# Moved and split steps at the start, in the scan and at the end of a Mamba-2 plus mixture-of-experts kernel

## The chip, the core and the metric

The kernel runs on one core of one Trainium2 chip. The metric is the device time of one execution in microseconds. Engines are called TensorE (PE; PEld is its weight loads), VectorE (DVE), ScalarE (ACT), GpSimd (POOL) and SyncE (SP); each works through its own queue in the order in which the program lists its instructions.

## The reference

Two stages follow each other. The first is a chunked state-space scan over 4 batches, 8 heads, 768 tokens, head size 32, state size 16:

```python
cum = np.cumsum(la, axis=-1)
L = np.exp(cum[:, :, :, None] - cum[:, :, None, :]) * causal
y_intra = einsum('bhij,bhjd->bhid', (C @ B.T) * L, x)
y_inter = einsum('bhin,bhnd->bhid', C, state) * np.exp(cum)[..., None]
state = decay_full * state + sum_j(B_j x_j * decay_from_j)
```

The second stage routes the 3072 resulting rows of 256 numbers to 8 experts by the largest cosine logit, and computes

```python
h = np.maximum(x[mask] @ w1[e], 0.0)
out[mask] = gate_w[mask, None] * (h @ w2[e])
```

with hidden size 1024; gate_w is the softmax value of the chosen expert. All is float32.

## The kernel before

The order of all work around the change is written out by hand: the program is recorded under a manual schedule, so the order of the calls is the order on each engine's queue.

**The scan.** It goes over NC = 6 chunks of Q = 128 tokens, all batches and heads together. For each chunk c, `spread_decays` (line 208) spreads the decays over the partitions by TensorE, into columns 384 to 512 of the PSUM tile `pg`; `scale_c` (268) multiplies them into C and gives `cp`; `mask_c` makes two masked copies on ScalarE. `inner(c, j)` (371) computes the scores of two batches (j = 0 for batches 0 and 1, j = 1 for 2 and 3) into columns 0 to 384 of `pg`, and `mask_inner(c, j)` (387, instruction line 391) multiplies the causal mask in on VectorE and gives `g`. As there is one `pg`, `inner(c, 1)` waits for the mask of (c, 0). `from_states` (397), `outputs` (408, line 419) and `first_outputs` (426, line 432) add up the outputs in the PSUM banks `py`: from the carried state, from the second 64 tokens with the scaled inputs `xs`, and from the first 64 tokens with `xb`. `xs` and `xb` are made on GpSimd (`scale_x` 290, `scale_first_half` 302) from `rT`, the turned inverse decays (`turn_inverses` 247). `sums`, `add_sums` and `decay_states` keep the state: products into the banks `pz`, `V` and the decayed `T` on VectorE. `between` (316) makes the factors between chunks, `wb` and `wm`. `keep_outputs` copies `py` to SBUF on ScalarE, and `finish` (452) turns the rows through `pz` and `py`, computes the logits with the turned expert embedding (`turn_emb`, `scale_emb`), and the rows go to DRAM.

In a chunk, `first_outputs` of all four batches stands behind `outputs(c, 1)`, which needs the mask of (c, 1). In the head of `mamba` (824), chunk 1's decays go to `pg` after chunk 0's have been read, then comes one warm-up matmul; on VectorE `scale_emb` stands ahead of the first mask, and `scale_c(1)` and `between` behind it, ahead of the second mask.

**The end of the scan.** `scan_end` (971) begins the first expert's first rows (`first.up`, `first.down`; each `f` is a 128 block of the hidden size) while the last chunk's rows are ranked within their experts. `rank_rows` is a small product, `keep_ranks` a copy, `places` a row of small VectorE operations, `locate` products that gather row indices in `pz`. `end_places` finishes the table, from which GpSimd gathers the rows of the job `late`.

**The experts.** The eight experts, the last six of them sorted by their number of rows, run as jobs, most of them with first-layer and second-layer products built from sums of blocks (lines 1244 and 1316). The last job has 364 rows in four tiles of `tr` = 104 (the last has 52). Its second layer is in `moe_end` (1505): `down(j, half)` computes 128 of the 256 output columns for rows 0 to 208 (half 0) or 208 to 364 (half 1), with one matmul pair for each of 8 values of f. Each `out(i)` turns a tile of rows back on TensorE (line 1361), scales it with the gate (1364 on ScalarE, 1366 on VectorE), and scatters it with an indirect DMA of GpSimd (1367).

Loads come by SyncE's queue in the order of the calls: a, then ct, bi, x, xa, b of chunk 0, then the same of chunk 1; later ones wait until their buffer is free (two buffers each).

Of the kernel before, what the change touches and what calls it, by code (L numbers as in the profile page):

```python
# [12 lines left out]
ALU = mybir.AluOpType  # L13
# [165 lines left out]
def warm_up(k, n):  # L179
    for _ in range(n):  # L180
        k.nc.tensor.matmul(k.pz[1][:], lhsT=k.warm[:, 0:Q], rhs=k.warm[:], start=True, stop=True)
# [23 lines left out]
    tt(out=v, in0=v, in1=w[:, 1].unsqueeze(3).to_broadcast([128, 2, 2, SQ]), op=ALU.mult)  # L205


def spread_decays(k, c):

    for b in range(NB):  # L210
        r = slice(32 * b, 32 * b + 32)
        k.nc.tensor.matmul(
            k.pg[:, b, 384:512], lhsT=k.spread[r, c % 4, :], rhs=k.f[r, c // 4, 0:Q], start=True, stop=True,
            tile_position=(32 * b, 0),
        )


# [50 lines left out]
def scale_c(k, c):  # L268


    t = k.ld[c]
    t.cp = k.work.tile([128, NB, 5, HQ], F32, name="cp", tag="cp")
    k.nc.vector.tensor_tensor(
        out=t.cp[:, :, 0:2, :].rearrange("p b j s -> p b (j s)"), in0=t.ct[:], in1=k.pg[:, :, 384:512], op=ALU.mult
    )
# [147 lines left out]
                    )  # L423


def first_outputs(k, c, zs=range(KD)):
    t = k.ld[c]
    for b in range(NB):
        for z in zs:
            for r in range(2):  # L430
                q, o = 2 * z + r, 64 * r
                k.nc.tensor.matmul(  # L432
                    k.py[z][o : o + 64, Q * b : Q * b + HQ],
                    lhsT=k.xb[c % 2][:, b, q].rearrange("p v d -> p (v d)"), rhs=t.g[b // 2][:, q, b % 2, 0:HQ],
                    start=False, stop=True, tile_position=(0, o), skip_group_check=True,
                )
# [127 lines left out]
def turn_emb(k, ps):  # L564


    nc = k.nc
    for z in range(KD):
        nc.tensor.transpose(ps[:, E * z : E * z + E], k.en2[:, z, :], k.ident[:E, :E])
    nc.scalar.copy(out=k.emb_t[:, :, 0:E], in_=ps[:, 0 : KD * E].rearrange("p (z e) -> p z e", z=KD))  # L570
# [253 lines left out]
def mamba(k):  # L824
    nc = k.nc
    k.f = k.mc.tile([128, 2, Q], F32, name="f")
    k.fe = k.mc.tile([128, 2, 3], F32, name="fe")
    k.rT = k.mc.tile([128, 2, 2, 128], F32, name="rT")
    k.V = k.mc.tile([128, NB, 2 * D], F32, name="V")
    k.ends = k.mc.tile([128, 8, NB, 3], F32, name="ends")  # L830
    k.rr, k.wm = {}, {}
    for c in range(NC):
        k.ld[c] = Net()
        k.ld[c].g = []
    load_decays(k)
    expert_emb(k)
    load(k, 0)
    build_consts(k)
    warm_up(k, 12)
    decays(k)  # L840
    load(k, 1)
    square_emb(k)
    clear_first_half(k, 0)
    clear_first_half(k, 1)
    route_consts(k)
    spread_decays(k, 0)
    warm_up(k, 3)
    split_b(k, 0)
    scale_c(k, 0)
    mask_c(k, 0)  # L850
    inverses(k, 0)
    block_ends(k)
    scale_emb(k)
    spread_decays(k, 1)
    warm_up(k, 1)
    inner(k, 0, 0)
    mask_inner(k, 0, 0)
    turn_inverses(k, 0, k.py[0][:, 0:256])
    scale_x(k, 0, nc.gpsimd)
    scale_first_half(k, 0, nc.gpsimd)  # L860
    scale_c(k, 1)
    spread_ends(k, k.pz[0][:, 0:96])
    between(k, 1, NC)
    turn_emb(k, k.pz[1][:, 400:416])

    for c in range(NC):
        t = k.ld[c]
        n = c + 1
        if c == 0:
            load(k, 2, ("ct", "x", "xa", "b", "bi"))  # L870
        elif c + 2 < NC:
            load(k, c + 2, ("x",))
        if 2 <= c < NC - 1:
            spread_decays(k, n)
        if 2 <= c < NC - 1:
            add_sums(k, c)
        if c >= 2:
            inner(k, c, 0)
        if c == NC - 1:
            finish(k, c - 1, (0,))  # L880
            early_places(k, c - 3)
        if c >= 2:
            mask_inner(k, c, 0)
# [12 lines left out]
        if 1 <= c < NC - 1:  # L896
            scale_c(k, n)
        if c >= 2:
            pick(k, c - 2)
        if c > 0:  # L900
            finish(k, c - 1, (2,) if c == NC - 1 else (1, 2) if 3 <= c else (0, 1, 2))
            keep_rows(k, c - 1)
            if c < NC - 1:
                send_rows(k, c - 1)
        inner(k, c, 1)
        mask_inner(k, c, 1)
        if c > 0 and n < NC:
            decay_states(k, n)
        if c > 0 and c + 2 < NC:
            load(k, c + 2, ("bi", "xa"), t.masked)  # L910
        if c == 0:
            sums(k, 0)
        if n < NC:
            split_b(k, n)
            mask_c(k, n)
            pass_c(k, n)
        if c == NC - 1:
            k.early_x = half_rows(k)
            gather_tiles(k, k.early_x, k.gi0, 0, 3 * NB * Q)
        if c >= 2:  # L920
            count_picks(k, c - 2)
        if c == NC - 1:
            add_located(k, c - 3)
        if c == 0:
            scale_first_half(k, n, nc.gpsimd, (0,))
        elif n < NC:
            scale_first_half(k, n, nc.gpsimd, after=t.paired)
        if 3 <= c < NC - 1:
            add_located(k, c - 3)
        if c > 0:  # L930
            from_states(k, c)
        if c >= 2:
            rank_rows(k, c - 2)
            keep_ranks(k, c - 2)
        outputs(k, c, 0)
        if c == 0:
            spread_decays(k, 2)
            inner(k, 1, 0)
            add_sums(k, 0)
            decay_states(k, 1)  # L940
            mask_inner(k, 1, 0)
        for zs in ((0,), (1,)) if c == NC - 1 else (range(KD),):
            outputs(k, c, 1, zs)
            first_outputs(k, c, zs)
            keep_outputs(k, c, zs)
        if c > 0 and c + 2 < NC:
            load(k, c + 2, ("b",), t.kept)
        if c == NC - 2:
            load_first_w1(k, 1, t.kept)
        if c == NC - 1:  # L950
            hold(k, send_rows(k, c - 1), t.kept)
            load_weights(k, 0, (1,), t.kept)
        if c + 2 < NC:
            sums(k, n)
        if c == 2:
            turn_inverses(k, 1, k.pz[0][:, 0:256])
        if c == NC - 1:
            pick(k, c - 1)
            count_picks(k, c - 1)
        if c >= 2:  # L960
            places(k, c - 2)
        if c == 4:
            shift_places(k)
        if c == 1:
            inverses(k, 1)
        if c == 0:
            scale_first_half(k, n, nc.gpsimd, (1,))
            place_consts(k)


def scan_end(k):
# [12 lines left out]
    gather_tiles(k, whole.x[:, 0:HT], k.gi0, NT, 3 * NB * Q)  # L984
    for f in range(3):
        first.up(f)
    locate(k, c - 2, True, False)
    first.up(3)
    rank_rows(k, c)
    keep_ranks(k, c)  # L990
    places(k, c)
    locate(k, c - 1, False, False)
    gates.square(0)
    first.up(4)
# [2 lines left out]
    for f in (5, 6, 7):  # L997
        first.up(f)
    locate(k, c, False, True)
    first.down(0, fs=range(2))  # L1000
    late = end_places(k, whole)
    first.down(0, fs=range(2, KF))
    gates.largest()
    gates.scale()
    gates.exp()
# [103 lines left out]
class Job:  # L1109
# [52 lines left out]
        else:  # L1162
            nc.vector.tensor_scalar_max(s.hT[:, f, 0:m], t, 0.0)

    def down(s, j, half=None, fs=range(KF)):
        k, nc, m = s.k, s.k.nc, s.cols
        if j == 0 and not half:
            s.yT = s.tile([128, KD, s.nt * s.tr], "yoT", 2 if s.p is None else 1)
        h = s.nt // 2 * s.tr
        r = slice(0, m) if half is None else slice(h * half, h + (m - h) * half)  # L1170
        if fs[0] == 0:
            s.yp = s.bank("yp", 4)
        t = s.yp[:, r]
        for f in fs:
            nc.tensor.matmul(  # L1175
                t, lhsT=s.w2[:, f, 128 * j : 128 * j + 128], rhs=s.hT[:, f, r], start=(f == 0), stop=(f == KF - 1)
            )
        if fs[-1] < KF - 1:
            return
        if j % 2 == 0 or s.bank_ is not None:  # L1180
            nc.scalar.copy(out=s.yT[:, j, r], in_=t)
        else:
            nc.vector.tensor_copy(out=s.yT[:, j, r], in_=t)
# [320 lines left out]

def moe_end(k, j):

    j.down(0, 0)
    j.down(1, 0)
    for i in range(2):
        j.down(0, 1, range(4 * i, 4 * i + 4))  # L1510
        j.out(i)
    j.down(1, 1)
    j.out(2)
    j.out(3)


def leftover_blocks(k):
# [243 lines left out]
```

## Time and profile before

| what | us |
|---|---|
| median of 3 runs (250.78 to 251.99) | 251.48 |
| the profiled execution | 251.42 |
| its span from first to last instruction | 249.7 |
| TensorE matmuls busy | 235.6 (94%) |
| VectorE / ScalarE / GpSimd busy | 183.3 / 125.8 / 123.0 |
| mean granted TensorE clock | 0.995 |

The page lists for each engine its busy time, and in another part the chain of work that ended last: followed back from the last instruction, at each step to what released it. In a row of the timeline the first number is the start and the second the time of a group of instructions, then come engine, line, operation, output and input with sizes; in brackets stands the idle time of the engine before it and what ended it. "DMA" as releaser means that the data had not landed. SPq is SyncE's queue issuing a transfer.

### The profile page before, as it was taken

To read this page: it belongs to the slowest core of one execution; us is meant where nothing else is said; L and a number is where in the kernel's file an instruction comes from. 1 tells how busy PE (TensorE), PEld (TensorE's weight loads), DVE (VectorE), ACT (ScalarE), POOL (GpSimd) and SP (SyncE) were. 2 spreads that over 40 slices of the span, in tenths; PEclk is the share of its full clock that TensorE was granted. 3 is DMA by queue.
4 is the path that set the end of the run, shared out by engine and by line. 5 is a ranking of instruction groups with operands and counts; after the bars stand their busy time and mean duration, and the time that the engine had idled before them with its cause. 6 is when DMAs were issued, how large, how long until landed. Compare 5 with 4: busy or idle time off the path is not lost.

```text
span 249.7 us, 6977 instructions
## 1 busy us (share of the span) xinstructions
PE 235.6 (94%) x2675; PEld 214.7 (86%) x2675; DVE 183.3 (73%) x476; ACT 125.8 (50%) x361; POOL 123.0 (49%) x161
## 2 busy tenths in 40 slices
PE   7779999999999999999999999999999999999990
PEld 2567787788789799999999999989998999999890
DVE  6894788988965647688968878897897986883121
ACT  3446478764363543752773385166358437528300
POOL 5898454462536583711484176157427516026033
PEclk9999999999999999999999999999999999999998
DMA  4995775663292699996821942672294202001001
GB/s 116 296 253 192 209 248 177 195 178 87 88 285 66 158 296 225 275 270 173 241 65 47 257 141 73 162 209 68 48 262 152 53 0 58 8 0 51 14 21 41
DMA packets 22548, 35.93 MB, mean 144 GB/s; under 512 B 2777, under 2 KB 15780, under 8 KB 22512
## 3 DMA queue, kind: packets, MB, share of 16 engines
q1 hardware_dynamic: 19264, 28.73, 41.9%
q0 software_dynamic: 3088, 6.67, 9.6%
q8 instruction: 22, 0.36, 0.6%
q14 instruction: 14, 0.11, 0.1%
q10 hardware_dynamic: 160, 0.06, 0.1%
HBM read 29.05 MB, written 6.50 MB: 142 GB/s over the span
## 4 chain that ended last, share of the span: by engine, by line
PE 68%; issue 10%; DVE 8%; DMA 7%; ACT 3%; POOL 2%; POOLq 1%; DVEq 0%; SPq 0%; ACTq 0%
PE yp L1316 19%; PE yp L1244 11%; PE hp L1244 8%; DMA out_dram<-yo,to 5%; PE pg L381 5%; DVE g L391 4%; PE py L432 3%; PE eb L1157 2%; PE hp L1157 2%; PE yp L1175 2%; PE py L419 2%; PE yp L1144 2%; POOL out_dram L1367 2%; PE pz L449 1%; PE py L449 1%
## 5 line engine op out<-in xcount | busy, mean ns | idle before, releaser
L1367 POOL DMA_INDIRECT out_dram<-yo,to x32 | 34.4, 1074 | 60.5 <-ACT yo L1364 43.0
L1047 POOL DMA_INDIRECT xg<-y_rows,gi x26 | 31.9, 1225 | 12.3 <-issue 6.9
L1262 ACT ACTIVATE hT<-hT 128x416 f32<-128x416 f32 (+5 forms) x42 | 22.4, 535 | 11.0 <-DVE hT L1266 8.3
L1316 PE MATMUL yp<-T,S 128*128 128x208 f32 (+4 forms) x144 | 26.4, 333 | 0.0
L391 DVE TENSOR_TENSOR g<-pg,mask 128x1536 f32<-128x1536 f32 x12 | 21.1, 1755 | 6.7 <-PE pg L381 6.5
L1266 DVE TENSOR_TENSOR hT<-hp,u 128x416 f32<-128x416 f32 (+5 forms) x28 | 15.7, 567 | 13.9 <-PE hp L1244 6.5
L1316 PEld LDWEIGHTS yp<-T,S 128*128 128x128 f32 x144 | 24.6, 190 | 0.0
L1244 PE MATMUL yp<-T,S 128*128 128x208 f32 (+5 forms) x112 | 21.3, 333 | 0.1
L1257 ACT COPY p<-yp 128x416 f32<-128x416 f32 (+5 forms) x14 | 6.7, 481 | 28.2 <-PE yp L1244 28.2
L1395 POOL TENSOR_TENSOR gr<-gr,half 104x4 f32<-104x4 f32 (+2 forms) x8 | 9.6, 1199 | 22.4 <-ACT sq L1389 22.3
L1244 PEld LDWEIGHTS yp<-T,S 128*128 128x128 f32 x112 | 18.3, 190 | 0.6 <-ACT u L1257 0.4
L1316 PE MATMUL yp<-hT,w 128*128 128x208 f32 (+4 forms) x96 | 18.2, 333 | 0.0
L1175 PE MATMUL yp<-hT,w 128*128 128x208 f32 (+1 forms) x96 | 16.4, 326 | 0.5 <-ACT hT L1262 0.5
L293 POOL TENSOR_TENSOR xs<-x,rT 128x1024 f32<-128x1024 f32 x6 | 11.8, 1969 | 10.2 <-issue 6.4
L1316 PEld LDWEIGHTS yp<-hT,w 128*128 128x128 f32 x96 | 16.5, 190 | 0.0
L1175 PEld LDWEIGHTS yp<-hT,w 128*128 128x128 f32 x96 | 15.6, 190 | 0.8 <-ACT hT L1262 0.8
L1257 ACT COPY u<-yp 128x416 f32<-128x416 f32 (+5 forms) x28 | 13.6, 488 | 2.8 <-PE yp L1244 2.5
L1213 DVE TENSOR_TENSOR T<-hT 128x832 f32<-128x832 f32 (+4 forms) x12 | 11.9, 990 | 3.6 <-ACT hT L1262 2.4
L1201 DVE TENSOR_TENSOR S<-w 128x512 f32<-128x512 f32 x14 | 9.5, 682 | 3.7 <-DMA w<-in_moe_w_dram 3.7
L444 ACT COPY yT<-py 128x512 f32<-128x512 f32 x12 | 6.5, 589 | 10.9 <-PE py L432 10.9
L1213 DVE TENSOR_TENSOR T<-hT,T 128x832 f32<-128x832 f32 (+4 forms) x12 | 11.9, 989 | 0.2
L381 PE MATMUL pg<-cp,bi 32*128 32x128 f32 x192 | 11.6, 299 | 0.0
(300 smaller groups left out, 589.0 us busy)
## 6 DMA issues: line engine op xcount, KB each, us to landing
w<-in_moe_w_dram SPq DMA_DIRECT2D x32, 256.0 KB
w<-in_moe_w_dram SPq DMA_DIRECT2D x8, 1024.0 KB
y_rows<-rows SPq DMA_DIRECT2D x6, 528.0 KB
x<-in_x_dram SPq DMA_DIRECT2D x6, 512.0 KB
ct<-in_CT_dram SPq DMA_DIRECT2D x6, 256.0 KB
bi<-in_BT_dram SPq DMA_DIRECT2D x6, 256.0 KB
b<-in_B_dram SPq DMA_DIRECT2D x6, 256.0 KB
xa<-in_x_dram SPq DMA_DIRECT2D x6, 128.0 KB
```

Source lines behind the costliest of these rows:

```text
L293: d = engine.tensor_tensor(out=t.xs[:].rearrange("p b (h d) -> p b h d", h=NH), in0=t.x[:].rearrange("p b (h d) -> p b h d", h=NH), in1=r_ ...
L381: t.paired = k.nc.tensor.matmul(k.pg[:, q, 192 * u + a : 192 * u + a + n], lhsT=m, rhs=x, start=True, stop=True, tile_position=(32 * q, 0),)
L391: t.masked = k.nc.vector.tensor_tensor(out=g[:], in0=k.pg[:, :, 0:384].rearrange("p q (u m) -> p q u m", u=2), in1=k.mask[:].unsqueeze(1). ...
L1047: k.nc.gpsimd.indirect_dma_start(out=x, out_offset=None, in_=k.y_d[0:rows, :], in_offset=bass.IndirectOffsetOnAxis(ap=at, axis=0), bounds_ ...
L1175: nc.tensor.matmul(t, lhsT=s.w2[:, f, 128 * j : 128 * j + 128], rhs=s.hT[:, f, r], start=(f == 0), stop=(f == KF - 1))
L1213: s.k.nc.vector.tensor_tensor(out=T[n], in0=x, in1=y, op=ALU.subtract)
L1244: nc.tensor.matmul(t[:, m * u : m * u + m], lhsT=w[:, f : f + 128], rhs=x, start=start and u == 0, stop=True, skip_group_check=True,)
L1257: nc.scalar.copy(out=p[:, 0 : 2 * m], in_=t[:, 0 : 2 * m])
L1262: nc.scalar.activation(h, h, ACT.Relu)
L1266: nc.vector.tensor_tensor(out=h, in0=view(t), in1=view(p), op=ALU.add)
L1316: nc.tensor.matmul(t, lhsT=a[:, f], rhs=b[:, f], start=start and f == 0, stop=(f == 3), skip_group_check=True)
L1367: d = nc.gpsimd.indirect_dma_start(out=k.out[:, :], out_offset=bass.IndirectOffsetOnAxis(ap=s.to[:p, i : i + 1], axis=0), in_=y[:p], in_of ...
```

## The change

Four things are done.

1. `first_outputs` takes a half j like `outputs`, and is called for j = 0 right after `outputs(c, 0)`, so ahead of `outputs(c, 1)` that needs the second mask; for j = 1 it stays where all of it was.
2. Chunk 1's decays go to columns 384 to 512 of the four banks `py` and `pz`, one batch in each, instead of to `pg`. `scale_c(1)` follows at once, as four VectorE operations of 128 columns, ahead of the first mask. The warm-up matmul behind the decays goes. `scale_emb` stands behind the first mask of chunk 0, and `between` and `turn_emb` behind the second.
3. In `scan_end`, `rank_rows`, `keep_ranks` and `places` of the last chunk stand ahead of `locate(c - 2)` and `first.up(3)`; the table follows after one f of `first.down` instead of two.
4. In `moe_end`, half 0 of the second layer goes through f in the order 4 to 7, 0 to 3. The second 128 columns of half 1 are computed for the third tile (104 rows) and the fourth (52 rows) apart; the third tile's output stands before the last two f of the fourth, and the fourth is scaled on ScalarE.

```diff
-def spread_decays(k, c):
+def spread_decays(k, c, to=None):
+    k.ld[c].spread = to
+    if to is None:
+        to = [k.pg[:, b, 384:512] for b in range(NB)]
     for b in range(NB):
...
-            k.pg[:, b, 384:512], lhsT=k.spread[r, c % 4, :], rhs=k.f[r, c // 4, 0:Q], start=True, stop=True,
-            tile_position=(32 * b, 0),
+            to[b], lhsT=k.spread[r, c % 4, :], rhs=k.f[r, c // 4, 0:Q], start=True, stop=True,
+            tile_position=(32 * b, 0), skip_group_check=True,
...
+    if t.spread is not None:
+        for b in range(NB):
+            k.nc.vector.tensor_tensor(
+                out=t.cp[:, b, 0:2, :].rearrange("p j s -> p (j s)"), in0=t.ct[:, b, :], in1=t.spread[b], op=ALU.mult
+            )
+        return
...
-def first_outputs(k, c, zs=range(KD)):
+def first_outputs(k, c, j, zs=range(KD)):
-    for b in range(NB):
+    for b in (2 * j, 2 * j + 1):
...
     block_ends(k)
-    scale_emb(k)
-    spread_decays(k, 1)
-    warm_up(k, 1)
+    spread_decays(k, 1, [t[:, 384:512] for t in k.py + k.pz])
+    scale_c(k, 1)
     inner(k, 0, 0)
     mask_inner(k, 0, 0)
     turn_inverses(k, 0, k.py[0][:, 0:256])
     scale_x(k, 0, nc.gpsimd)
     scale_first_half(k, 0, nc.gpsimd)
-    scale_c(k, 1)
+    scale_emb(k)
     spread_ends(k, k.pz[0][:, 0:96])
-    between(k, 1, NC)
-    turn_emb(k, k.pz[1][:, 400:416])
...
         if c == 0:
+            between(k, 1, NC)
+            turn_emb(k, k.pz[1][:, 400:416])
             sums(k, 0)
...
         outputs(k, c, 0)
+        first_outputs(k, c, 0)
...
             outputs(k, c, 1, zs)
-            first_outputs(k, c, zs)
+            first_outputs(k, c, 1, zs)
...
-    locate(k, c - 2, True, False)
-    first.up(3)
     rank_rows(k, c)
     keep_ranks(k, c)
     places(k, c)
+    locate(k, c - 2, True, False)
+    first.up(3)
...
-    first.down(0, fs=range(2))
+    first.down(0, fs=range(1))
     late = end_places(k, whole)
-    first.down(0, fs=range(2, KF))
+    first.down(0, fs=range(1, KF))
...
-    j.down(0, 0)
-    j.down(1, 0)
+    order = [4, 5, 6, 7, 0, 1, 2, 3]
+    j.down(0, 0, order, order)
+    j.down(1, 0, order, order)
     for i in range(2):
         j.down(0, 1, range(4 * i, 4 * i + 4))
         j.out(i)
-    j.down(1, 1)
+    a = 3 * j.tr
+    j.down(1, slice(2 * j.tr, a))
+    j.down(1, slice(a, j.cols), range(6))
     j.out(2)
-    j.out(3)
+    j.down(1, slice(a, j.cols), range(6, KF))
+    j.out(3, True)
```

`down` itself takes a slice of rows as `half`, and an order of f that sets which matmul starts and which ends the sum.

More of the change, by code (lines that the diff above doesn't have):

```diff
@@ L1163, in up, with down @@
             nc.vector.tensor_scalar_max(s.hT[:, f, 0:m], t, 0.0)
-    def down(s, j, half=None, fs=range(KF)):
+    def down(s, j, half=None, fs=range(KF), order=range(KF)):
         k, nc, m = s.k, s.k.nc, s.cols
@@ L1169, in down @@
         h = s.nt // 2 * s.tr
-        r = slice(0, m) if half is None else slice(h * half, h + (m - h) * half)
-        if fs[0] == 0:
+        if isinstance(half, slice):
+            r = half
+        else:
+            r = slice(0, m) if half is None else slice(h * half, h + (m - h) * half)
+        if fs[0] == order[0]:
             s.yp = s.bank("yp", 4)
@@ L1175, in down @@
             nc.tensor.matmul(
-                t, lhsT=s.w2[:, f, 128 * j : 128 * j + 128], rhs=s.hT[:, f, r], start=(f == 0), stop=(f == KF - 1)
+                t, lhsT=s.w2[:, f, 128 * j : 128 * j + 128], rhs=s.hT[:, f, r], start=(f == order[0]),
+                stop=(f == order[-1]),
             )
-        if fs[-1] < KF - 1:
+        if fs[-1] != order[-1]:
             return
```

## The prediction, on record before the change was run

> **What bounds the kernel now.** I read the chain of waits first: TensorE has 68% of it, VectorE 8%, "issue" 10%. From 83 to 232 us TensorE is busy almost throughout and the change touches nothing there; it works in three places: the start (8 to 26 us), each chunk's second half of scores (24 to 62 us), and the end of the scan and of the program (69 to 84 us and from 232 us). So I read the chain there, then the timeline of each engine.
>
> ```profile
> 10.13 1.76 DVE g L391
> 11.89 0.59 DVE cp L273
> 12.48 0.46 DVE wb L322
> 12.97 1.13 DVE wm L327 x2
> 14.10 1.67 DVE g L391
> ...
> 24.15 1.77 DVE g L391
> 25.96 0.65 PE py L419 x32
> 26.62 1.08 PE py L432 x32
> ```
>
> The start is a VectorE queue: the two masks of chunk 0 (`g`) with cp of chunk 1, wb and wm between them. Later a mask holds the chain while TensorE waits for it, and both output blocks stand behind it. The timeline tells why the queue is as slow as it is:
>
> ```profile
> 5.58 0.43 SPq L66 DMA_DIRECT2D ct<-in_CT_dram  x1
> 6.06 0.43 SPq L66 DMA_DIRECT2D bi<-in_BT_dram  x1
> 10.93 1.97 POOL L293 TENSOR_TENSOR xs<-x,rT 128x1024 f32<-128x1024 f32 x1 [0.61 <-ACT rT L253]
> 12.40 0.53 DVE L322 TENSOR_TENSOR wb<-ends 128x20 f32<-128x20 f32 x1
> 12.42 0.91 ACT L265 ACTIVATE bt<-bi,tmask 128x256 f32<-128x256 f32 x2 [0.69 <-DMA bi<-in_BT_dram]
> 12.97 1.13 DVE L327 TENSOR_SCALAR wm<-wb,tmask 128x20 f32<-128x20 f32 x2
> 15.16 1.97 POOL L293 TENSOR_TENSOR xs<-x,rT 128x1024 f32<-128x1024 f32 x1
> 16.19 1.22 DVE L339 TENSOR_TENSOR T<-V,wm 128x256 f32<-128x256 f32 x1
> ```
>
> To see: chunk 1's ct and bi are issued together, and ScalarE waits for bi until 12.42. The trace's marks of ct's completion, sixteen of them, run from 10.78 to 11.73. So ct of chunk 1 is there at 11.73, not before; cp at 11.81 just fails to wait for it. And wb, wm, T, a few hundred elements, last until a POOL operation ends (12.90, 13.93, 17.12).
>
> ```profile
> L228 PE MATMUL pz<-ends_in,spread x8: 188/269/269, 10.3 to 11.0; 128*128 128x24 f32 x8
> ...
> 232.58 6.95 PE L1175 MATMUL yp<-hT,w 128*128 128x208 f32 x40 [0.55 <-ACT hT L1262]
> 240.87 2.29 PE L1175 MATMUL yp<-hT,w 128*128 128x156 f32 x16
> ...
> 244.71 1.00 POOL L1367 DMA_INDIRECT out_dram<-yo,to  x1 [1.81 <-DVE yo L1366]
> 246.02 0.91 POOL L1367 DMA_INDIRECT out_dram<-yo,to  x1 [0.31 <-issue]
> ```
>
> At the end TensorE waits for a relu until 232.58, and the last output leaves 1.31 us behind the third, which is POOL's own pace.
>
> [...]T takes 1.22 here, 0.46 undisturbed at 35.0[...]L228, with only 24 columns streamed, steps by 0.112 us[...].
>
> **The change part by part** (against the profiled execution, span 249.67, time 251.42; that is 0.06 below the median 251.48).
>
> (1) Start. The decays of chunk 1 go to py and pz, and cp of chunk 1 becomes four instructions ahead of the first mask on VectorE's queue. They free nothing if ct isn't there: VectorE is done with ends_in at 8.98 and then waits until 11.78 instead of starting the mask at 10.13. Size of one: 512 columns take 0.68 and 1536 take 1.74, so 1.04 ns a column and 0.14 fixed, 0.27 for 128, stepping by about 0.20: four end at 12.6. First mask: 12.57 to 14.31 (before 10.13 to 11.89). Queued behind it on TensorE: inner(0,1), 1.18 (12.54 to 13.72): done 15.55. The emb operations (0.96) now stand there on VectorE[...]; between 15.3 and 16.2, I take 16.1. Second mask then 16.1 to 17.9; before, it ended at 15.76. The turned inverses use py0, so they wait for the first slice of cp (12.05): rT comes at 12.9 and POOL's xs at 13.03, before 10.93, +2.1. POOL's six operations then run back to back (8.56 us before, 10.93 to 19.49): 13.03 to 21.6.
>
> wb and wm now follow the second mask: wb is held until xs of chunk 1 ends (19.23), the first wm until the next (20.45), V is copied by 21.1, T is held until 21.6 and the mask of (1,0) runs 21.8 to 23.5 (before 17.33 to 19.07). V of chunk 1 is four operations, 0.78: 24.3. The turn of rows into pz1 waits for it and inner(1,1) stands about 1.0 behind (turns 0.22 twice, logits 0.3 twice): 25.3, where before it was 22.71. **+2.6**. Bounds: [...]the wait is TensorE's and ScalarE's alone: spread 0.32, inner(1,0) 0.89, outputs 0.58, first half of first outputs 0.54 behind a second mask that ends at 17.34, so keep_outputs at 19.75 instead of 19.36, **+0.4**. If ct lands 0.5 later or the tiny operations lose a further POOL operation (1.07): **+3.6**. I take +2.5. What the move gives (no warm-up of 0.32, emb off the queue before the first mask, decays without a wait) lies inside the wait for ct and is worth nothing. The DMA order on SP is unchanged up to chunk 2; x of chunk 2 is issued 2.1 later (it waits for POOL's xb), at 16.0, and needed at about 23.9: hidden.
>
> (2) First outputs split. A block of 32 output matmuls takes 0.58, one of first_outputs 1.08. Half of the latter, 0.54, now runs ahead of the wait for the second mask. It saves the idle time there and no more: block start plus 0.58 to the restart is 25.03+0.58 to 25.96, 34.37+0.58 to 35.14, 44.32+0.58 to 45.10, 54.24+0.58 to 55.03, so 0.35, 0.19, 0.20, 0.21. In chunk 5 there is no gap (63.65 is after nearly all of the mask, done at 64.01); yT of z=0 comes 0.27 later there, still before TensorE asks for it at 66.1. Sum **-0.95**; bounds -1.0 and -0.6, if a late xb of POOL holds one. In chunk 0 it stands inside the wait of (1).
>
> (3) Last ranks. rank_rows moves ahead of locate and up(3); it needs the one-hot picks, done at 71.20, and TensorE is there at 71.07: up to 0.2 lost. places then starts 1.1 earlier (its scalar copy at 71.6, not 72.64), but its result (75.31) was not waited for: TensorE asks at 75.72. So nothing gained. The table stands behind one f of down instead of two: 0.35, of which VectorE's add to idx_t (ends 76.51) leaves about 0.28. With it the gathers of late come earlier, for which TensorE waits at 82.19. Net **-0.1** (-0.3 to +0.1).
>
> (4) End. Starting with f 4 to 7 asks for relus done by 231.70; what is left is TensorE's drain (232.03) and two event waits: start 232.27, **-0.3**. Then 16 matmuls of 156 columns at 0.133 (2.14) become 16 of 104 and 16 of 52, all at the weight load's 0.112: the third tile's rows are turned after 28 of them, 3.13 after the start, against 2.80 before (VectorE's copy included: 240.77 to 243.57). Both turns then run together, 0.1 closer than before, so counted from its start the end stands about 0.45 longer until the third output: start 0.3 sooner, output at 244.85 for 244.71. The fourth is ready at about 245.9 (ScalarE scales it, 0.47) and POOL takes it at 246.16 instead of 246.02; from there the 3.65 us to the end are the same. **+0.15**. Bounds: -0.35 if loads hide under the 104 columns (0.09 each) and -0.1 more of the turns; +0.5 if the narrow ones cost load plus stream.
>
> Sum: +2.5 - 0.95 - 0.1 + 0.15 = +1.6. 251.42 + 1.6 = 253.0; against the median I state **252.9**.
>
> **Rivals.** *The start is absorbed* (the other side): T gets through between POOL operations and TensorE's chain alone counts, +0.4. Then +0.4 - 0.95 - 0.1 + 0.15 = -0.5: 250.9. For it: before, the chain from 16 to 22.7 runs through TensorE and ScalarE, not T. Against it: wb, wm and T each waited before, and POOL's row is unbroken after. It decides once T of chunk 1 ends before about 20 us. *ct lands in time*: by 9.5 us. Then the first mask stays at 10.1, the second starts behind inner(0,1) at about 13.05 instead of 14.02, and the sum is -0.95 - 0.95 - 0.1 + 0.15 = -1.85: 249.6. Against it: x (512 KB), xa and b stand ahead of ct in the same queue and DMA is full from 4 us on. *Worse*: start +3.6, end +0.5: 254.5; for it, every tiny VectorE operation meets a POOL operation of 1 to 2 us. That the change doesn't do what it says I exclude: the orders of instructions show it.
>
> **How the numbers follow.** Forecast 0.50 (its own range 252.2 to 253.8), absorbed 0.25, ct in time or more gained than counted 0.13, worse 0.12. One measurement tells about 0.5% from no change, so 250.2 to 252.7 counts as same. Of the forecast's half, 0.39 lies above 252.7 and 0.11 below; with 0.12 of "worse", slower is 0.51. Same is 0.11 + 0.25 = 0.36, less a little for absorbed cases with more gain: 0.35. Faster: 0.14. Range 250.4 to 254.2: it takes in the absorbed case and most of the worse one.
>
> **What would show it.** Right: VectorE idle ahead of the first of four cp (128x128), released by DMA ct at about 11.8; first mask at 12.6; xs on POOL at 13.0; T of chunk 1 longer than 0.46 and ending near 21.9; inner(1,1) after 25. No idle time ahead of L419 behind a mask in chunks 1 to 4. In the end, 128x104 and 128x52 both stepping 0.11 and the third output about 12.6 us after the start of the last second layer (before 12.1). Wrong: a first mask before 11 us, or the scan's first layer starting earlier than 68.8.

## The result and the profile after

The changed kernel takes 254.03 us (median of 20 runs, 251.66 to 257.04), the kernel before beside it 251.56 us (20 runs). The ratio is 1.0086, with a 95% interval of 1.0059 to 1.0113, so the change costs 1.5 to 2.8 us. The ratio, here and below, leaves out executions that took over 1.5% longer than the fastest of the same kernel (three of the changed kernel's 20). The profiled execution took 253.39 us with a span of 251.55 us (249.67 before), 1.88 us longer. The lines of the diff stand somewhat lower in the new program: L273 became L278 and L282, L391 became L400, L419 became L428, L432 became L441, L1175 became L1187, L1367 became L1380.

The timeline of the start, of the changed kernel, with the second half of chunk 1's scores and the first expert's first layer as its last two lines (start, time, engine, line, operation, in brackets the idle time before it and what ended it):

```profile
12.17 0.48 DVE L278 TENSOR_TENSOR cp<-ct,py 128x128 f32<-128x128 f32 x2 [3.52 <-DMA ct<-in_CT_dram]
...
12.61 0.66 PE L252 MATMUL py<-ident,rr 128*128 128x128 f32 x2 [2.90 <-DVE cp L278]
...
12.97 1.75 DVE L400 TENSOR_TENSOR g<-pg,mask 128x1536 f32<-128x1536 f32 x1
...
13.76 1.97 POOL L302 TENSOR_TENSOR xs<-x,rT 128x1024 f32<-128x1024 f32 x1 [3.39 <-ACT rT L256]
...
15.05 1.78 DVE L567 TENSOR_SCALAR en<-emb,emb_r 8x128 f32<-8x128 f32 x2
...
16.94 1.76 DVE L400 TENSOR_TENSOR g<-pg,mask 128x1536 f32<-128x1536 f32 x1
...
18.61 1.38 DVE L331 TENSOR_TENSOR wb<-ends 128x20 f32<-128x20 f32 x1
...
20.02 1.13 DVE L336 TENSOR_SCALAR wm<-wb,tmask 128x20 f32<-128x20 f32 x2
...
21.58 0.83 DVE L348 TENSOR_TENSOR T<-V,wm 128x256 f32<-128x256 f32 x1
...
22.34 1.74 DVE L400 TENSOR_TENSOR g<-pg,mask 128x1536 f32<-128x1536 f32 x1
...
25.98 0.33 PE L390 MATMUL pg<-cp,bt 32*128 32x64 f32 x2
...
70.70 2.38 PE L1166 MATMUL eb<-xT,w 128*128 128x208 f32 x12
```

The same work in the kernel before, where the prediction doesn't show it:

```profile
9.31 0.55 DVE L558 TENSOR_SCALAR en<-emb,emb_r 8x128 f32<-8x128 f32 x2
...
22.71 0.33 PE L381 MATMUL pg<-cp,bt 32*128 32x64 f32 x2
...
68.77 2.38 PE L1157 MATMUL eb<-xT,w 128*128 128x208 f32 x12
```

VectorE, TensorE and GpSimd all wait for one transfer, chunk 1's ct, which is complete at 12.08. The first mask, whose scores are done at 9.71, stands behind the four cp on VectorE's queue and starts at 12.97 (10.13 before), after 3.52 us in which VectorE waits for ct; GpSimd's first xs starts at 13.76 (10.93). Behind each mask small VectorE operations last until a GpSimd product ends: en takes 1.78 for twice 8x128 elements (0.55 before) and ends at 16.83, the product at 16.75; wb takes 1.38 (0.53 before) and ends at 19.99, the product at 19.95. The mask of chunk 1 starts 5.0 us later than before (17.33). The second half of chunk 1's scores starts at 25.98 for 22.71: **+3.27**. The chain of waits of the changed kernel goes through these operations between the second mask and the turn of rows into pz:

```profile
18.69 1.31 DVE wb L331
...
20.93 0.23 DVE wm L336
...
21.58 0.83 DVE T L348
...
24.00 0.85 DVE V L374 x4
24.90 0.44 PE pz L458 x2
```

One thing more is not a wait. These are stretches of TensorE in the same kernel (stretch, its length, busy time with the number of matmuls, granted clock as a share of full speed, DMA share, GB/s):

```profile
11.00:12.50 1.50, 0.00 (x0) 0.87 1.05 388
12.50:14.00 1.50, 1.39 (x8) 0.50 1.12 192
14.00:15.50 1.50, 1.50 (x16) 0.50 0.66 220
...
17.00:18.50 1.50, 1.50 (x57) 0.50 0.49 147
18.50:20.00 1.50, 1.50 (x52) 0.85 0.85 262
```

The clock falls to half from 12.12 on, for 6.83 us by the trace's own record. The second half of chunk 0's scores lies in it, and lasts 2.1 instead of 1.18 us. In the profile before, no stretch of the start is below full clock.

From there the changed kernel gains. The first expert's first layer starts at 70.70 for 68.77 (+1.93), the late rows are turned 1.76 later than before, the last second layer starts at 234.11 for 232.58 (+1.53), the third output leaves at 246.64 for 244.71 (+1.93). So up to the third output it is +3.27 at the start, -1.34 in chunks 1 to 5, -0.17 at the end of the scan, -0.23 ahead of the last second layer and +0.40 in it, together +1.93. The end of the program, in the timeline of the changed kernel:

```profile
234.11 6.93 PE L1187 MATMUL yp<-hT,w 128*128 128x208 f32 x40 [0.30 <-PEq L1615]
...
242.37 3.23 PE L1187 MATMUL yp<-hT,w 128*128 128x104 f32 x28
...
245.65 0.55 PE L1187 MATMUL yp<-hT,w 128*128 128x52 f32 x4
246.64 1.00 POOL L1380 DMA_INDIRECT out_dram<-yo,to  x1 [2.25 <-DVE yoT L1196]
247.94 0.92 POOL L1380 DMA_INDIRECT out_dram<-yo,to  x1 [0.31 <-issue]
```

The 28 narrow matmuls (some of 104, some of 52 columns) take 3.23, 0.115 each; their weight loads, on PEld, take 3.21 of it, also 0.115 each. The third output leaves 12.53 us after the start of this layer, before it was 12.13.

### The profile page after: what moved, and what is told of

Its sections match the earlier page's. It is cut to its first block, busy times and chain, and to the rows that moved or that the text cites. A ratio compares the mean times of both kernels' runs of the same rounds, so it can differ in the third digit from the quotient of the medians.

```text
span 251.6 us, 7014 instructions
## 1 busy us (share of the span) xinstructions
PE 239.8 (95%) x2690; PEld 218.9 (87%) x2690; DVE 184.2 (73%) x479; ACT 126.1 (50%) x362; POOL 123.2 (49%) x161
## 4 chain that ended last, share of the span: by engine, by line
PE 70%; issue 10%; DMA 8%; DVE 3%; ACT 3%; POOL 2%; SPq 1%; POOLq 1%; ACTq 0%; DVEq 0%
PE yp L1329 19%; PE yp L1257 11%; PE hp L1257 8%; DMA out_dram<-yo,to 5%; PE pg L390 4%; DMA ct<-in_CT_dram 3%; PE py L441 3%; PE py L428 2%; PE hp L1166 2%; PE yp L1187 2%; PE py L411 2%; PE yp L1153 2%; POOL out_dram L1380 2%; PE eb L1166 2%; PE pz L458 1%
## 5 line engine op out<-in xcount | busy, mean ns | idle before, releaser
L1380 POOL DMA_INDIRECT out_dram<-yo,to x32 | 34.4, 1074 | 60.8 <-ACT yo L1377 43.0
L1275 ACT ACTIVATE hT<-hT 128x416 f32<-128x416 f32 (+5 forms) x42 | 22.4, 535 | 11.0 <-DVE hT L1279 9.2
L400 DVE TENSOR_TENSOR g<-pg,mask 128x1536 f32<-128x1536 f32 x12 | 21.1, 1755 | 4.3 <-PE pg L390 4.1
L1187 PE MATMUL yp<-hT,w 128*128 128x208 f32 (+3 forms) x112 | 17.9, 314 | 0.3 <-PEq L1615 0.3
L1187 PEld LDWEIGHTS yp<-hT,w 128*128 128x128 f32 x112 | 17.1, 191 | 0.5 <-ACT hT L1312 0.5
L1329 PEld LDWEIGHTS yp<-hT,w 128*128 128x128 f32 x96 | 16.5, 190 | 0.0
L1257 PE MATMUL yp<-T,w 128*128 128x208 f32 (+5 forms) x56 | 11.2, 344 | 0.3 <-ACT u L1270 0.2
```

What stands on the lines that cost most here:

```text
L400: t.masked = k.nc.vector.tensor_tensor(out=g[:], in0=k.pg[:, :, 0:384].rearrange("p q (u m) -> p q u m", u=2), in1=k.mask[:].unsqueeze(1). ...
L1187: nc.tensor.matmul(t, lhsT=s.w2[:, f, 128 * j : 128 * j + 128], rhs=s.hT[:, f, r], start=(f == order[0]), stop=(f == order[-1]),)
L1257: nc.tensor.matmul(t[:, m * u : m * u + m], lhsT=w[:, f : f + 128], rhs=x, start=start and u == 0, stop=True, skip_group_check=True,)
L1275: nc.scalar.activation(h, h, ACT.Relu)
L1329: nc.tensor.matmul(t, lhsT=a[:, f], rhs=b[:, f], start=start and f == 0, stop=(f == 3), skip_group_check=True)
L1380: d = nc.gpsimd.indirect_dma_start(out=k.out[:, :], out_offset=bass.IndirectOffsetOnAxis(ap=s.to[:p, i : i + 1], axis=0), in_=y[:p], in_of ...
```

## The experiments

Ten kernels were run. The table has the ratio of many runs to the kernel before, and how many of these runs had a low mean clock (below 0.985); then what one profile of each shows: when ct of chunk 1 was complete, when the second half of chunk 1's scores and the first expert's first layer started, and how long TensorE had half its clock between 10 and 25 us.

| kernel | ratio, 95% interval | low clock | ct | scores | layer | half clock |
|---|---|---|---|---|---|---|
| before | 1 | 39 of 152 | 11.73 | 22.71 | 68.77 | none |
| changed | 1.0086, 1.0059 to 1.0113 | 15 of 17 | 12.08 | 25.98 | 70.70 | 6.83 |
| start_alone | 1.0115, 1.0013 to 1.0218 | 4 of 4 | 10.98 | 25.51 | 71.87 | 6.83 |
| rest_alone | 0.9962, 0.9937 to 0.9988 | 4 of 20 | 11.58 | 22.70 | 68.31 | 3.41 |
| ct_first | 1.0019, 0.9979 to 1.0058 | 9 of 12 | 7.56 | 23.45 | 68.54 | 6.83 |
| filled | 1.0064, 1.0039 to 1.0090 | 9 of 20 | 12.07 | 27.07 | 72.26 | 6.83 |
| between_back | 1.0029, 1.0004 to 1.0055 | 16 of 20 | 10.20 | 23.05 | 68.05 | 3.41 |
| ct_and_between | 1.0000, 0.9977 to 1.0023 | 12 of 20 | 9.47 | 24.72 | 70.46 | 6.83 |
| end_unsplit | 0.9962, 0.9935 to 0.9989 | 7 of 20 | 11.40 | 24.06 | 69.15 | 3.41 |
| rest_filled | 0.9986, 0.9959 to 1.0012 | 0 of 19 | 12.30 | 24.40 | 71.03 | 3.41 |
| split_alone | 0.9970, 0.9947 to 0.9993 | 5 of 22 | 11.22 | 21.97 | 66.55 | none |
| rest_ct_sooner | 0.9938, 0.9912 to 0.9965 | 3 of 20 | 9.67 | 22.36 | 67.51 | 3.41 |

One profile is one draw: ct's completion alone differs by 2.1 us between kernels that load it in the same place. The profiled execution is also far from the middle in some kernels: it is the fastest of all runs of ct_first (251.46, median 253.09) and of between_back (250.90, median 253.08), the slowest of filled (255.13, median 253.73) and the slowest but one of ct_and_between and rest_filled. So the ratios decide; a profile shows a way in which the time can come about, not how often it does.

### The start, and the rest

start_alone makes part 2 alone; rest_alone makes parts 1, 3 and 4:

```diff
-    scale_emb(k)
-    spread_decays(k, 1)
-    warm_up(k, 1)
+    spread_decays(k, 1, [t[:, 384:512] for t in k.py + k.pz])
+    scale_c(k, 1)
...
-    scale_c(k, 1)
+    scale_emb(k)
     spread_ends(k, k.pz[0][:, 0:96])
-    between(k, 1, NC)
-    turn_emb(k, k.pz[1][:, 400:416])
...
+            between(k, 1, NC)
+            turn_emb(k, k.pz[1][:, 400:416])
             sums(k, 0)
```

> Only part 2 of the change is made: the decays and cp of chunk 1 early, scale_emb and between later; the other three parts are as before. My theory (the start costs what the two traces show at the second half of chunk 1's scores, and nothing behind it takes it back): that block starts at about 26.0 us instead of 22.7, the first layer of the first expert about 3.2 later than before at 72.0, and the time is 251.5 + 3.2 = 254.7, ratio 1.013 (1.010 to 1.015). Rival (part of the loss is swallowed by gaps in the later chunks, and the gain that I put down to the split of first_outputs is really this): the block is at 26.0 but the first layer starts only about 2 later, 70.8, and the time is 253.5, ratio 1.008.

> Part 2 is undone, parts 1, 3 and 4 are kept. My theory: the start is that of before (second half of chunk 1's scores at 22.7, TensorE's clock whole in every slice), each of chunks 1 to 4 gains its gap, the first layer of the first expert starts at about 67.6 (before 68.8), the end is +0.16 and the ranks are -0.1 to -0.2: time 251.5 - 1.2 = 250.3, ratio 0.995 (0.992 to 0.998). Rival (the split gains only behind a late start, since late POOL products hold the first halves otherwise): first layer at 68.6 to 68.8, ratio 0.999 to 1.001.

The ratios say that the start costs and the rest gains: 1.0115 and 0.9962, and the two together come near the whole (1.0077 for 1.0086). The cost of the start is best seen from the change against rest_alone, which differs from it in the start alone: 1.0086 for 0.9962, about 3.1 us, with intervals far apart. start_alone's own interval, from four runs, is too wide to tell my 1.013 from the rival's 1.008; its profile has the first layer 3.10 later than before with the scores 2.80 later, so in this profile nothing of the start is swallowed in the chunks. Without the start the other parts gain 0.3 to 1.6 us, which excludes the rival's 0.999. Two details of rest_alone's expectation failed in its profile: the clock was at half for 3.41 us, and the first layer started at 68.31, not 67.6.

start_alone also shows what part 3 does. Without it TensorE waits for the gathered rows of the late job; here in the timeline of the kernel before, then of start_alone:

```profile
82.20 0.49 PE L1144 MATMUL eb<-ident,next_x 104*128 104x104 f32 x3 [0.58 <-DMA next_x<-y_rows,gi]
```

```profile
84.65 0.31 PE L1152 MATMUL eb<-ident,next_x 104*128 104x104 f32 x1
86.01 0.49 PE L1152 MATMUL eb<-ident,next_x 104*128 104x104 f32 x3 [1.05 <-DMA next_x<-y_rows,gi]
```

The three kernels without part 3 wait 0.58 (before), 1.05 and 0.96 us there (split_alone). Of the nine with it, four don't wait, four wait 0.17 to 0.35 and one 0.82 (rest_filled). In the changed kernel the wait is gone.

### Is it the wait for ct?

ct_first takes the changed kernel and loads chunk 1's ct ahead of chunk 0's x:

```diff
-    load(k, 0)
+    load(k, 0, ("ct", "bi"))
+    load(k, 1, ("ct",))
+    load(k, 0, ("x", "xa", "b"))
...
-    load(k, 1)
+    load(k, 1, ("bi", "x", "xa", "b"))
```

> The changed kernel, with the load of chunk 1's ct taken ahead of those of x, xa and b of chunk 0 in SyncE's queue, so that it lands some 2 to 3 us sooner; x lands about 1 us later. First theory (the wait for ct is the whole cost, as my rival in the prediction had it): cp at about 9.0, first mask at 10.1, xs at 10.9, second half of chunk 1's scores at about 21.8, time 249.6, ratio 0.992. Second theory ([...]as wb and wm now stand behind the second mask): mask and xs as above, but T of chunk 1 lasts until GpSimd's six products are done at about 19.5, the block starts at 23.0 to 23.5, and the time is 250.4 to 250.8, ratio 0.996 to 0.997. Third (the wait was cheap[...]): block at 25 or later, ratio over 1.003.

The timeline of ct_first, VectorE and GpSimd:

```profile
8.80 0.28 DVE L278 TENSOR_TENSOR cp<-ct,py 128x128 f32<-128x128 f32 x1
...
9.87 1.76 DVE L400 TENSOR_TENSOR g<-pg,mask 128x1536 f32<-128x1536 f32 x1 [0.40 <-POOL T L598]
...
10.60 1.97 POOL L302 TENSOR_TENSOR xs<-x,rT 128x1024 f32<-128x1024 f32 x1 [0.23 <-ACT rT L256]
...
15.52 1.31 DVE L331 TENSOR_TENSOR wb<-ends 128x20 f32<-128x20 f32 x1
...
18.40 0.83 DVE L348 TENSOR_TENSOR T<-V,wm 128x256 f32<-128x256 f32 x1
```

The first mask and xs are even earlier than before, and still the scores start at 23.45, 0.74 later than before. wb and T again last until GpSimd products end (wb to 16.83, the product to 16.78; T to 19.23, the product to 18.95), but here they don't hold the scores. The chain of waits of ct_first runs through TensorE from 11.69 on, apart from one copy on ScalarE:

```profile
11.69 2.08 PE pg L390 x32
...
13.99 1.01 PE pz L358 x32
...
17.65 1.32 PE pg L390 x32
```

Until 18.44 TensorE does this at half clock. So the block stands in the window of the second theory (23.0 to 23.5), but not for its reason. The first theory is out: with ct in time the change isn't at 0.992. The ratio, 1.0019, lies above the second theory's 0.996 to 0.997, which is outside its interval, and the interval reaches the third theory's 1.003. Sooner ct takes 0.0067 off the change's ratio, about 1.7 us, with intervals that just don't overlap.

### Is it the order of the tiny operations?

between_back leaves ct where it is and puts scale_emb, between and turn_emb back; ct_and_between does both:

```diff
+    scale_emb(k)
     spread_decays(k, 1, [t[:, 384:512] for t in k.py + k.pz])
     scale_c(k, 1)
...
-    scale_emb(k)
     spread_ends(k, k.pz[0][:, 0:96])
+    between(k, 1, NC)
+    turn_emb(k, k.pz[1][:, 400:416])
...
-            between(k, 1, NC)
-            turn_emb(k, k.pz[1][:, 400:416])
             sums(k, 0)
```

> The changed kernel with scale_emb ahead of chunk 1's decays and between and turn_emb ahead of the second mask again, where they were before; the decays stay in py and pz and cp ahead of the first mask, so the wait for ct stays. If the wait for ct is the larger half of the start's cost: second half of chunk 1's scores at about 24.8 to 25.3 us (25.98 with the change, 22.71 before), time 253.3, ratio 1.006. If the move of emb and between behind the masks is the larger half (wb, wm and T then each wait for one of GpSimd's products late in the row): the block at 23.8 to 24.4, time 252.3, ratio 1.002 to 1.004.

> Both repairs: chunk 1's ct loaded ahead of x, and emb and between where they were before. What is left of the change's start is the decays in py and pz and cp ahead of the first mask. If these two causes are all of it: first mask at 9.9 to 10.1, second mask at 13.0 to 13.7 (14.02 before), second half of chunk 1's scores at 22.2 to 22.8, time 250.0 to 250.4 with a whole clock, ratio 0.994 to 0.996, and the clock is whole about as often as in the kernel before. If a third cost is there (TensorE waits for cp before it can turn the inverses, or the clock drops in every run whatever the order is): the block at 23.2 or later, ratio 0.998 or more.

between_back gains 0.0057 on the change, and the two intervals don't overlap: the order of the small operations is worth about 1.4 us of the start. The ratio lies where the expectation put it if the order were the larger half (1.002 to 1.004), but the interval reaches nearly to the 1.006 of the other case. The profile can't decide, since ct happened to be complete at 10.20 in that execution, the fastest of the 20. The timeline of between_back:

```profile
13.67 1.13 DVE L336 TENSOR_SCALAR wm<-wb,tmask 128x20 f32<-128x20 f32 x2
...
16.89 1.22 DVE L348 TENSOR_TENSOR T<-V,wm 128x256 f32<-128x256 f32 x1
```

wm now ends ahead of the second mask, and T meets one GpSimd product, as before the change; neither is on this profile's chain of waits any more. With both repairs the kernel is at 1.0000, 0.0086 below the change, but 0.0038 above the kernel with the old start. So the two repairs together take away the larger part of the start's cost, not all of it, and less than the sum of each alone (0.0057 and 0.0067). This is the expectation's case of a third cost: the scores at 24.72, after 23.2, and a ratio not under 0.998. The remainder of about 1 us, if it is real (the two intervals just overlap), is what is left of the change: decays in four other banks and cp ahead of the first mask. In the profile of ct_and_between xs waits 1.14 us for x, which ct was put ahead of, and half the clock lasts 6.83 us. Its chain of waits runs through TensorE from 12.17 to 24.72, apart from one copy on ScalarE and a pause of 0.69, and 12 of its 20 runs have the low clock, against 4 of 20 of rest_alone. That speaks for the clock as the third cost; the two are not separated.

### Is it the clock?

filled gives TensorE of the changed kernel 20 matmuls of ones to do while it waits for ct; rest_filled gives 14 to rest_alone, where TensorE waits for cp:

```diff
     inner(k, 0, 0)
+    fill(k, 20)
     mask_inner(k, 0, 0)
```

> The changed kernel with 20 matmuls of 128 columns of ones put behind the first half of chunk 0's scores, into columns that nobody reads, so that TensorE is busy from 9.7 to about 12 us while it waits for ct. Clock theory (TensorE's idle stretch of 2.9 us made its clock drop to half from 13 to 19 us, and that is why the start cost 3.27 instead of the 2.6 that I worked out): the clock stays whole in every slice, the eight products into pz take 1.0 instead of 1.75, the second half of chunk 0's scores 1.2 instead of 1.9, the second mask ends 0.7 to 1.4 sooner, the second half of chunk 1's scores starts at 25.3 instead of 26.0, and the time is about 0.6 below that of the change, ratio to before 1.006. Rival (VectorE and GpSimd set the pace, TensorE's clock only fills idle time): the clock stays whole, but T of chunk 1 still ends at 22.0 to 22.4 and the block starts at 25.8 to 26.0, ratio 1.008 to 1.009.

> As the run with the start undone, with 14 matmuls of 128 columns of ones where TensorE waits for cp of chunk 1 (11.46 to 12.54 us before), into a bank that is free then. Clock theory (it is idle time of TensorE at 10 to 13 us that makes its clock drop to half for some 3 to 7 us; the kernel before escapes in about half of its runs): nearly all runs have a mean clock of 0.99 or more, none is at 0.98, the median falls from 250.7 to 250.5 and the highest run from 252.8 to 251.5; ratio 0.994. Rival (whether the clock drops is set outside this stretch, or by chance alone): clocks spread as in the run without it, ratio 0.996 to 0.997.

Neither settles it. In filled the 20 matmuls end at 11.25 and TensorE still waits 1.34 us for cp. The clock still falls to half, only later (at 16.11, again for 6.83 us), so the profile fits neither theory: the scores start at 27.07. With the clock whole until 16.11 the second mask starts at 16.50 for 16.94 and T ends at 22.15 for 22.41, so by these two profiles a whole clock is worth some 0.3 to 0.4 us up to there. The ratio of 1.0064 is the clock theory's 1.006, but its interval overlaps that of the change. In rest_filled the clock part of the expectation came true: 15 of 19 runs have a mean of 0.99 or more and none is below 0.985, where rest_alone has 10 and 4 of 20. Yet the time doesn't fall: the ratio is 0.9986 for 0.9962. Its profile shows a gather wait of 0.82 us and, at 33.37, TensorE pausing 1.11 us with the mark "issue" (below); that these are the cause isn't shown.

What can be said of the clock is an association. In the twelve profiles a mean clock of 0.992 or more goes with no half clock at the start, 0.985 to 0.991 with 3.41 us of it and less with 6.83 us (rest_filled's own, at 0.991, has 3.41). Sorted by these marks, 152 runs of the kernel before have medians of 251.26 us (45 runs), 251.84 (68) and 253.46 (39), so it kept the whole clock in fewer than the half of its runs that rest_filled's expectation speaks of. The changed kernel has none, 2 and 15 of its 17 runs in the three classes. If the steps of 0.6 and 2.2 us are the price of the half clock, the change pays 1.2 us more of it on average than the kernel before; that is an estimate of the clock's share in the ratio, and it may overlap with the two causes above, since a longer wait of TensorE can go with both the lower clock and the longer time. Over all kernels the low clock goes with the new start: 9 of 20 runs or more in every kernel that has it in any form, 7 of 20 or fewer in those with the old one. The two kernels that should have shown the price by removing the cause didn't.

### The other parts

split_alone makes part 1 alone. end_unsplit is rest_alone with the last 156 rows in one piece:

```diff
-    a = 3 * j.tr
-    j.down(1, slice(2 * j.tr, a))
-    j.down(1, slice(a, j.cols), range(6))
+    j.down(1, 1)
     j.out(2)
-    j.down(1, slice(a, j.cols), range(6, KF))
-    j.out(3, True)
+    j.out(3)
```

> Part 1 alone: first_outputs split around the second mask, everything else as in the kernel before. If the gaps behind the masks are what it gains (0.35, 0.19, 0.20, 0.21 in chunks 1 to 4, and nothing else): first layer of the first expert 0.95 sooner than before relative to the start of chunk 1's second half, time 251.5 - 0.95 = 250.6, ratio 0.996, and the three parts together (0.9962 measured) are no better than this one. If ranks and end help too: this part alone is at 0.998 or more. If the pauses of TensorE[...] move with it, single chunks differ from these gaps by up to 0.5 us either way, but the sum stays between -0.6 and -1.4.

> As the run with the start undone, but the last 156 rows stay one piece in the last second layer: only the order of f is kept of part 4. My theory (the pieces of 104 and 52 columns cost 0.4 us as both are bound by the weight load): the third output leaves 12.1 us after the last second layer's start, as before the change, against 12.5 with the pieces; the end is 0.25 sooner than before instead of 0.16 later; time 0.4 below the run with the pieces, 250.3 for 250.7, ratio to before 0.994 to 0.995. Rival (the fourth tile's output on GpSimd sets the end, and the pieces bring it no later): the same time as the run with the pieces within 0.1.

Part 1 alone is at 0.9970, a gain of 0.2 to 1.3 us, and all three parts at 0.9962: the two can't be told apart. In its profile the way from chunk 1's scores to the first layer is 1.48 shorter than before, outside the 0.6 to 1.4 of the expectation. The gain is not where I had put it. Chunk 3 by TensorE's timeline, first of the kernel before, then of the changed one:

```profile
44.31 1.47 PE L419 MATMUL py<-g,xs 128*32 128x64 f32 x64
45.71 1.15 PE L432 MATMUL py<-g,xb 128*64 128x64 f32 x32
46.80 0.65 PE L349 MATMUL pz<-xs,b 128*32 128x64 f32 x32
...
49.52 0.49 PE L449 MATMUL py<-ident,yT 128*128 128x128 f32 x3 [0.49 <-issue]
```

```profile
47.00 0.65 PE L428 MATMUL py<-g,xs 128*32 128x64 f32 x32
47.58 0.69 PE L441 MATMUL py<-g,xb 128*64 128x64 f32 x16
48.20 0.65 PE L428 MATMUL py<-g,xs 128*32 128x64 f32 x32
48.78 0.69 PE L441 MATMUL py<-g,xb 128*64 128x64 f32 x16
49.40 0.65 PE L358 MATMUL pz<-xs,b 128*32 128x64 f32 x32
```

The output blocks run without a gap, as foreseen, but they take 2.40 us (47.00 to 49.40) for 2.49. Sixteen matmuls of first_outputs take 0.62 and not 0.54, half of 32. Over chunks 1 to 4 the blocks shrink from 2.60, 2.43, 2.49 and 2.45 to 2.40 each: 0.37 in all. The larger gain is that pauses of TensorE vanish which have no partner in the change: 0.49 "issue" in chunk 3 above, 0.34 "issue" in chunk 5 (at 63.65), and some 0.3 in chunk 2 ahead of the products of locate. Such pauses come and go with the kernel: the way from scores to layer is 46.06 us before and 46.36 in start_alone, and between 44.6 (split_alone) and 46.6 (rest_filled) in the ten kernels with part 1. So one profile can't price the split.

end_unsplit has the third output 12.10 us after the start of the layer (232.77 to 244.87), rest_alone 12.53 (231.92 to 244.45): the pieces cost 0.43 in the profile, as worked out. In the ratios the two are equal, 0.9962, as the rival had it, but the 0.0017 that the pieces would be worth is below what these intervals tell.

The last kernel is end_unsplit with chunk 1's ct loaded behind chunk 0's x and ahead of its xa and b:

```diff
-    load(k, 0)
+    load(k, 0, ("ct", "bi", "x"))
+    load(k, 1, ("ct",))
+    load(k, 0, ("xa", "b"))
```

> As the run with the start undone and the last 156 rows in one piece, and chunk 1's ct loaded ahead of xa and b of chunk 0 (behind x), so that it lands about 1 us sooner. Theory of the landing time (in the kernel before, cp at 11.8 is ready for ct at 11.7, and in runs in which ct lands later, up to 12.3, the second mask and all behind it shift): the median falls from 251.4 to about 251.0, the spread of the runs narrows by some 0.5 us at its upper end, ratio to before 0.994 to 0.995. Rival (the spread comes from the clock and from TensorE's pauses[...] alone): same as that run, 0.996.

It is the best of all, 0.9938: about 1.6 us below the kernel before, 3.7 below the change. The time of the theory was met, its spread not: the runs reach from 248.56 to 253.59 us, no narrower than those of end_unsplit (250.15 to 253.82). The intervals of the two overlap, and the kernel's own interval reaches the rival's 0.996, so the gain of the sooner ct by itself is likely, not shown.

## Why the prediction came out as it did

The direction (slower, above its own mark of 252.7) and the range held: 252.9 forecast, 254.03 measured, range 250.4 to 254.2. By its steps:

**(1) The start, +2.5: measured +3.27 in the profile.** In the profile the chain was right link by link: VectorE waits for ct ahead of four cp, the inverses wait for cp, en, wb, wm and T are held by GpSimd's row, and the turn of rows into pz1 waits for V. (The 0.46 of T at 35.00, which I called undisturbed, has a GpSimd product beside it until 35.17.) Each link came later than worked out: mask at 12.97 for 12.57, xs at 13.76 for 13.03, second mask at 16.94 for 16.1, mask of (1,0) at 22.34 for 21.8, scores at 25.98 for 25.3. The mis-sized terms are the landing of ct (12.08, I took 11.73 as a fixed number from one trace) and TensorE's time, which I took at full clock: the turn of the inverses took 0.66 for 0.44, inner(0,1) 2.1 for 1.18. The first two make up 0.6 of the 0.73 by which xs was late. The third did little by itself: the scores ended at 16.87 and en at 16.83, so en would have held the second mask anyway.

**(2) The split of first outputs, -0.95: the place was right, the size wrong both ways.** The gaps are gone, but each block of 16 costs 0.08 more than half of 32, so 0.37 remains. The scan still gained 1.34, since pauses that I had not connected with the change went away. That the sum came near is luck: the start was 0.77 dearer than forecast, and these pauses gave 0.39 of it back.

**(3) The last ranks, -0.1: measured -0.17 in the profile.** The reason was the right one: the table earlier, the gathers earlier. The wait of 0.58 that I mentioned is gone. Without part 3 it isn't fixed: 1.05 in start_alone, and 0.96 in split_alone, whose start isn't late. This I did not price.

**(4) The end, +0.15: measured +0.17.** The earlier start was 0.23 for 0.3, a step 0.115 for 0.112, the third output 12.53 after the start for 12.6.

**The rivals.** "Absorbed" fell: T of chunk 1 ended at 22.4, not before 20. "ct in time" gave 249.6, and ct_first, which makes ct come in time, has 1.0019. The step of that rival that fails in ct_first's profile is the second mask at 13.05: it starts at 13.84, since inner(0,1) takes 2.1 us at half clock, and TensorE, not the small operations, is late from there on. "Worse", 254.5, is nearest to the median: its reason (each tiny operation meets a product) was right in the changed kernel's profile, its end +0.5 wrong.

Of the 1.1 us between 252.9 and 254.03, the profiled executions account for 0.5 (they differ by +1.97 for the sum's +1.6, and 0.1 is rounding); the rest lies between the changed kernel's profiled execution (253.39) and its median.

## What to carry to other kernels

Putting cp ahead on VectorE's queue gave nothing here before its last input was there: VectorE waited 3.52 us for ct, with the first mask behind cp. When the margin is 0.1 us against a landing that differs by 2.1 us between kernels, price both sides of it. Before moving small operations on VectorE, look at what GpSimd runs at the new place: here en (1.78 for twice 8x128 elements) and wb (1.38 for 128x20) lasted until a GpSimd product had ended, and took 0.55 and 0.53 in the kernel before. And before naming what a wait costs, look whether the chain passes it: in ct_first's profile the same operations were about as slow (en 1.71, wb 1.31, T 0.83) and weren't on the chain, since TensorE was later. And count what the split itself costs: a half block of first_outputs took 0.62 here, where the whole one took 1.08.

## What the runs showed of the hardware that I had not expected

**Half clock for 3.41 or 6.83 us.** In all twelve traces TensorE's clock at the start is either whole or at half for 3.41 or 6.83 us, the second twice the first. With the change it fell at 12.12, 2.4 us after TensorE's last matmul (9.71) and ahead of the next one (12.61); in rest_alone at 13.51, after a longest wait of 1.08 us, while the kernel before kept its clock with the same wait of 1.08; in filled at 16.11, in a wait of 0.69 and after waits of 1.34 and 0.79. So the length of a wait alone doesn't tell, and what makes the clock fall isn't shown.

**Pauses with the mark "issue".** Some idle time of TensorE carries this mark: it waits for nothing that the profile shows. The timeline of end_unsplit has the largest, in the middle of sixteen equal matmuls:

```profile
16.44 0.32 PE L390 MATMUL pg<-cp,bi 32*128 32x128 f32 x1
18.00 0.81 PE L390 MATMUL pg<-cp,bi 32*128 32x128 f32 x7 [1.24 <-issue]
```

This pause stands behind TensorE's 221st matmul. In before (0.32), start_alone (0.97) and ct_and_between (0.69) one stands behind the same matmul, the 449th of TensorE's recorded instructions with weight loads and waits for semaphores counted. In rest_filled the 1.11 us at 33.37 stand behind number 1217, and in before the 0.49 of chunk 3 behind number 2241: 449 and 3 or 7 times 256. But the 0.34 of chunk 5 in before stands behind number 2936, which does not fit, and at most places that would fit there is no pause. The part of the page on DMA queues, of the kernel before:

```profile
q8 instruction: 22, 0.36, 0.6%
```

These are 22 packets of 16384 bytes. In the kernel before the first of them is done at 16.43 and TensorE goes on at 17.81, 1.38 us later; the eighth is done at 48.01 and TensorE goes on at 49.52, 1.51 later. That the pauses are waits for these packets isn't shown. The pauses named here are 0.32 to 1.24 us, and the same work lies at another count when an edit adds or removes instructions ahead of it. So I take it, as an estimate, that an edit can show more or less than its own cost by as much as such a pause.
